# Decode-attention backward: the last quarter of dV of heads 7, 14 and 21 stored as two partition ranges

## The chip, the cores and the metric

The kernel runs on one core of one Trainium2 chip. The metric is the device time of one execution in microseconds (us); lower is better. Times of the kernel before are the median of three runs; the profile is of one further execution, whose own time stands beside its span in the table below.

## The reference

The reference is the forward and backward pass of softmax attention with a single query row per head: 32 heads, 8192 keys, head width 128, everything in bf16.

```python
def _fwd_reference(q, k, v):
    scale = q.shape[-1] ** -0.5
    scores = jnp.einsum('bhqd,bhkd->bhqk', q, k) * scale
    attn = _softmax(scores, axis=-1)
    return jnp.einsum('bhqk,bhkd->bhqd', attn, v)
...
    _out, _vjp = jax.vjp(_f, q, k, v)
    _grads = _vjp(grad_out)
    return (_out0, *[jnp.asarray(_g) for _g in _grads])
```

The shapes are q and grad_out (1, 32, 1, 128), k and v (1, 32, 8192, 128). The outputs are the attention output, dq, dk and dv. Because there is one query row, dv of a head is an outer product, the 8192 softmax weights times the 128 values of grad_out, and dk is the outer product of the 8192 score gradients and q. Each of K, V, dK and dV is 2 MB for a head and 67 MB for all 32 heads, so the kernel must read 134 MB and write 134 MB.

## The kernel before, in words

A head's 8192 rows lie on the 128 partitions, 64 consecutive rows on each, so that one partition holds 64 x 128 bf16, which is 16 KB, contiguous in the chip's main memory too. K, V, dK and dV tiles all have the shape 128 x 64 x 128 and are moved whole: one transfer of 128 rows of 16 KB each. A "quarter" is 16 of the 64 rows of every partition, 128 pieces of 4 KB.

The loop at L307 runs over 33 rounds. Round h computes the forward part of head h (scores from K, softmax, dP from V) and the outer product dv of head h; it also finishes the backward part of head h-1 and the outer product dk of head h-1. `outer` (L250) makes one quarter of such an outer product with one VectorE instruction (L257) into the tile `G`; the tiles G_dv and G_dk have two buffers each, so the VectorE instruction for head h writes a buffer that the store of head h-2 must have left. After the fourth quarter the whole tile is stored with one transfer (L267). Only heads 0 and 31 are stored in two halves.

The order on each engine is the order in which the program is written (a manual schedule). All bulk transfers are issued by SyncE (SP), one after the other; each issue waits for its own condition and holds back those behind it. In a middle round SP issues: `load_k(h + 2)` (L81), the store of dk of head h-1 (L267), `load_v(h + 2)` (L85, written at L387 ahead of the fourth `outer(h, "dv", 3)` at L388), and the store of dv of head h (L267). SP's transfers take eight completion semaphores in turn, so that a transfer also waits until the eighth transfer before it has landed.

Every transfer is spread over the core's 16 DMA engines; each engine works through its own queue of packets in the order of issue, and puts a completion mark of its own on the transfer's semaphore. A transfer has landed when all sixteen marks are there. K tiles have three buffers, V tiles two.

Of the kernel before, what the change touches and what calls it, by code (L numbers as in the profile page):

```python
# [19 lines left out]
K_BUFS = 3  # L20
V_BUFS = 2
QD = 32


@with_exitstack
def kernel(
# [11 lines left out]
    nc = tc.nc  # L38
    P = 128
# [3 lines left out]
    NCH = NT // CH  # L43
    NQ = P // QD
    assert NCH == 4 and NQ == 4
    W = D // 2
    NB = W // QD
    scale = float(D) ** -0.5
# [20 lines left out]
    def rows_of(x, h, c, parts):  # L69
        L = NT // parts  # L70
        return x[0, h].rearrange("(p n) d -> p n d", p=P)[:, c * L:(c + 1) * L, :]

    def slots(X, c, parts):
        L = NT // parts
        return X[:, c * L:(c + 1) * L, :]
# [26 lines left out]
    nc.vector.memset(ones_f[:], 1.0)  # L102
    do_win = consts.tile([P, H, 2, QD + 2], BF16)
    nc.gpsimd.memset(do_win[:], 0.0)  # L104
    wins = {}
    for which in ("p", "ds"):
        wins[which] = []
        for i in range(2):
            w = consts.tile([P, NG, 2 * QD - 4], BF16, name=f"win_{which}{i}")
            nc.gpsimd.memset(w[:], 0.0)  # L110
# [5 lines left out]
    q_blk = consts.tile([P, H, 2 * NB, NQ], BF16)  # L116
    four = consts.tile([H, 2 * NB, NQ, QD], BF16)
    for w in range(NB):
        for e2 in range(2):
            nc.vector.tensor_copy(  # L120
                four[:, 2 * w + e2], rows[:, 0, :].rearrange("h (w j e) -> h w e j", w=NB, e=2)[:, w, e2:e2 + 1, :]
                .to_broadcast([H, NQ, QD]))
    tp = psT.tile([P, 2 * TB, P], BF16, tag="T", name="tp_q")
# [126 lines left out]
    def outer(h, which, r):  # L250
        x = st[h]
        if r == 0:
            x[which] = gpool.tile([P, NT, D], BF16, tag=which, name="G_" + which)
        G, dst = x[which], out_2 if which == "dk" else out_3
        rep, row = x["ds"] if which == "dk" else x["p"], x["qd"][:, 0 if which == "dk" else 1, :]
        Q = NT // 4
        nc.vector.tensor_tensor(  # L257
            slots(G, r, 4).rearrange("p n (a b) -> p n a b", b=R),
            slots(rep, r, 4).unsqueeze(2).to_broadcast([P, Q, D // R, R]),
            row.rearrange("p (a b) -> p a b", b=R).unsqueeze(1).to_broadcast([P, Q, D // R, R]),  # L260
            op=ALU.mult)
        parts = 1
        if h == 0 or h == H - 1:
            parts = 2
        if r % (4 // parts) == 4 // parts - 1:
            c = r // (4 // parts)
            nc.sync.dma_start(rows_of(dst, h, c, parts), slots(G, c, parts))  # L267
# [39 lines left out]
    for h in range(H + 1):  # L307
# [14 lines left out]
        if h > 0:  # L322
            ds_of(p_)
            outer(p_, "dk", 0)
            dq_of(p_, 0)
# [3 lines left out]
        if h > 0:  # L329
            dq_of(p_, 1)  # L330
            outer(p_, "dk", 1)
            if p_ % ST == ST - 1:
                gather_copy("ds")
                gather(p_, "ds", st[p_]["m"])
# [9 lines left out]
        if h > 0:  # L344
            outer(p_, "dk", 2)
# [80 lines left out]
```

## Time and profile before

| what | value |
|---|---|
| median of three runs | 644.06 us (644.03 to 644.63) |
| the profiled execution, its own time | 644.45 us |
| its span, first to last instruction | 642.7 us |
| moved in the span | 269.24 MB, mean 419 GB/s |
| VectorE busy | 537.9 us (84%) |
| TensorE matmul busy | 404.0 us (63%) |
| ScalarE busy | 194.4 us (30%) |
| stores of dv, issue to landing, median | 34.8 us |

The page of a profile gives busy times by engine, then the span cut into 40 slices, the DMA queues, the chain of work that ended last, the costliest groups of instructions and the DMA issues. A view by stretches gives, for any stretch of the span, the mean busy share of the 16 DMA engines and the rate in GB/s; a share of 1.00 means that all sixteen were busy throughout. The trace also keeps the sixteen completion marks of every transfer with their times, without the number of the engine that made them, and the start, length and size of every packet.

### The profile page before, as it was taken

The numbers are of one execution on the slowest core, as the hardware profiler recorded it, in microseconds if no ns is written. First come the engines' busy times: TensorE is split into PE (matmuls) and PEld (weight loads), VectorE is DVE, ScalarE is ACT, GpSimd is POOL, SyncE is SP. The second block draws the span as 40 slices with busy tenths as digits, with TensorE's granted clock in tenths as the row PEclk, the third lists the DMA queues.
The fourth block names the chain that finished last, engine by engine and source line by source line (L and its number), as shares of the span: only waits on it lengthen the run. The fifth ranks groups of instructions, "written<-read, shape, count | busy, mean of one in ns | idle before, by whom it ended". The sixth has DMA issues, their size and how long they took to land.

```text
span 642.7 us, 12069 instructions
## 1 busy us (share of the span) xinstructions
PE 404.0 (63%) x5128; PEld 289.2 (45%) x5128; DVE 537.9 (84%) x780; ACT 194.4 (30%) x475; POOL 5.9 (1%) x11
## 2 busy tenths in 40 slices
PE   2766667776755865458675577645687555765571
PEld 1544445455443543346553445433465343553350
DVE  6899999987988789788798888898878988789871
ACT  2333333332233331234232333213332133331240
POOL 3000000000000000000000000000000000000000
PEclk9888887775778666877577876668866678765775
DMA  8999999999999999999999999999999999999995
GB/s 346 410 428 430 424 428 429 427 425 430 428 425 420 423 426 428 429 429 428 429 430 426 429 430 423 433 428 429 430 423 433 426 428 430 429 428 427 429 390 209
DMA packets 19686, 269.24 MB, mean 419 GB/s; under 512 B 2353, under 2 KB 2353, under 8 KB 2865
## 3 DMA queue, kind: packets, MB, share of 16 engines
q1 hardware_dynamic: 19584, 268.47, 98.4%
q8 instruction: 40, 0.66, 0.4%
q14 instruction: 14, 0.11, 0.0%
q10 hardware_dynamic: 48, 0.01, 0.0%
HBM read 134.23 MB, written 134.23 MB: 418 GB/s over the span
## 4 chain that ended last, share of the span: by engine, by line
DMA 70%; DVE 24%; ACT 2%; PE 1%; issue 1%; POOL 0%; DVEq 0%; POOLq 0%
DMA out_dram<-G_dv 70%; DVE G_dv L257 14%; DVE XK_sb L157 4%; DVE G_dk L257 3%; ACT XV_sb L189 1%; DVE dpT L215 1%; DVE four L120 1%; ACT p_rep L368 0%; DVE sm L174 0%; PE acc_ds L232 0%; POOL do_win L104 0%; PE m_ps L246 0%; PE s_ps L168 0%; DVE ds L288 0%; PE T_ps L198 0%
## 5 line engine op out<-in xcount | busy, mean ns | idle before, releaser
L257 DVE TENSOR_TENSOR G_dv<-p_rep,qd 128x2048 bf16<-128x2048 bf16 x128 | 148.2, 1220 | 54.7 <-DMA out_dram<-G_dv 45.5
L198 PE MATMUL T_ps<-ident_f,Vt 128*128 128x128 f32 x1024 | 162.4, 318 | 0.5 <-DMA Vt<-in_v_dram 0.5
L257 DVE TENSOR_TENSOR G_dk<-ds_rep,qd 128x2048 bf16<-128x2048 bf16 x128 | 155.7, 1219 | 1.2 <-DVE ds_rep L292 0.2
L157 DVE STREAM_TRANSPOSE XK_sb<-Kt 128x1024 f32<-128x1024 f32 x128 | 151.4, 1221 | 4.3 <-DMA Kt<-in_k_dram 4.0
L198 PEld LDWEIGHTS T_ps<-ident_f,Vt 128*128 128x128 f32 x1024 | 144.7, 171 | 17.8 <-ACT XV_sb L189 13.6
L189 ACT COPY XV_sb<-T_ps 128x512 f32<-128x512 f32 x256 | 137.0, 590 | 24.0 <-PE T_ps L198 22.8
L280 PE MATMUL m_ps<-pd,ones_f 128*128 128x1 f32 x64 | 18.7, 361 | 162.9 <-DVE prod L218 162.9
L280 PEld LDWEIGHTS m_ps<-pd,ones_f 128*128 128x128 f32 x64 | 16.0, 311 | 168.8 <-DVE prod L218 154.0
L168 PE MATMUL s_ps<-q_blk,XK_sb 128*128 128x4 bf16 x2048 | 59.8, 168 | 22.9 <-DVE pdt L286 17.6
L168 PEld LDWEIGHTS <-XK_sb 128*128 128x128 bf16 x2048 | 57.1, 104 | 25.8 <-DVE pdt L286 20.2
L232 PE MATMUL acc_ds<-Kt,win_ds 128*32 128x512 bf16 x512 | 67.3, 627 | 0.9 <-ACT win_ds L293 0.9
L293 ACT COPY win_ds<-ds 128x64 bf16<-128x64 bf16 x32 | 7.8, 244 | 197.5 <-DVE ds L288 197.5
L355 ACT ACTIVATE e<-s_ps,nbias 128x64 f32<-128x64 f32 x32 | 10.0, 313 | 133.4 <-DVE nbias L350 133.4
L208 PE MATMUL dp_ps<-XV_sb,do_win 128*32 128x512 bf16 x512 | 34.3, 383 | 24.9 <-ACT XV_sb L189 24.9
L232 PE MATMUL acc_p<-Vt,win_p 128*32 128x512 bf16 x512 | 33.5, 382 | 0.0
L208 PEld LDWEIGHTS <-do_win 128*32 128x32 bf16 x512 | 14.2, 94 | 36.3 <-issue 29.7
L276 ACT CAST qd<-s_ps 128x256 bf16<-128x256 f32 x32 | 11.9, 372 | 43.4 <-PE s_ps L272 43.2
L215 DVE STREAM_TRANSPOSE dpT<-dp_ps 128x512 f32<-128x512 f32 x32 | 21.6, 675 | 0.0
L184 PEld LDWEIGHTS s_ps<-sm,lane 128*32 128x32 f32 x256 | 10.4, 151 | 17.6 <-DVE sm L174 16.7
L343 PEld LDWEIGHTS m_ps<-ident_f,top 128*128 128x128 f32 x32 | 5.8, 182 | 27.3 <-DVE top L341 26.3
L174 DVE TENSOR_TENSOR sm<-s_ps,in_quad 128x256 f32<-128x256 f32 x32 | 13.6, 425 | 4.5 <-PE s_ps L168 2.0
L232 PEld LDWEIGHTS <-win_p 128*32 128x32 bf16 x512 | 10.7, 96 | 12.7 <-ACT win_p L369 2.9
(55 smaller groups left out, 224.0 us busy)
## 6 DMA issues: line engine op xcount, KB each, us to landing
Vt<-in_v_dram SPq DMA_DIRECT2D x32, 2048.0 KB, 32.7
Kt<-in_k_dram SPq DMA_DIRECT2D x31, 2048.0 KB, 30.0
out_dram<-G_dv SPq DMA_DIRECT2D x30, 2048.0 KB, 34.8
out_dram<-G_dk SPq DMA_DIRECT2D x30, 2048.0 KB, 32.3
out_dram<-G_dv SPq DMA_DIRECT2D x4, 1024.0 KB, 13.6
out_dram<-G_dk SPq DMA_DIRECT2D x4, 1024.0 KB, 13.0
Kt<-in_k_dram SPq DMA_DIRECT2D x4, 512.0 KB, 5.2
out_dram<-fin_sb SPq DMA_DIRECT2D x2, 8.0 KB, 13.5
```

The source lines that it names most:

```text
L157: nc.vector.transpose(XK[h][:, :, :, u, :], slots(Kt[h], u, NCH).rearrange("p g d -> p (g d)").bitcast(F32).rearrange("p (g w j) -> p g w ...
L168: nc.tensor.matmul(out[:, g, :], lhsT=cols[:, g, c // 2, c % 2], rhs=q_blk[:, h, c, :], start=(c == 0), stop=(c == 2 * NB - 1), skip_group ...
L174: nc.vector.tensor_tensor(x["sm"][:], x["s"][:, 0:NT].rearrange("p (a g) -> p a g", a=NQ).unsqueeze(2) .to_broadcast([P, NQ, NCH, CH]), in ...
L184: nc.tensor.matmul(x["s"][a * QD:(a + 1) * QD, 128:128 + NT], lhsT=lane[:], rhs=x["sm"][:, a].rearrange("p u g -> p (u g)"), start=True, s ...
L189: nc.scalar.copy(XV[h][:, c * TB:(c + 1) * TB, :], st[h].pop(("T", c))[:])
L198: nc.tensor.transpose(T_ps[:, i, :], words[:, m * P:(m + 1) * P], ident_f[:])
L208: nc.tensor.matmul(out[b * QD:(b + 1) * QD, :], lhsT=do_win[:, h, e2, 2 - 2 * z:2 - 2 * z + QD], rhs=cols[:, z, e2, :, b * QD:(b + 1) * QD ...
L215: nc.vector.transpose(x["dpT"][:].rearrange("p m r -> p (m r)"), x["dp"][:])
L232: nc.tensor.matmul(acc[which][b * QD:(b + 1) * QD, :], lhsT=window(h, which)[:, g, at:at + QD], rhs=X[:, 4 * g:4 * g + 4, :].rearrange("p ...
L257: nc.vector.tensor_tensor(slots(G, r, 4).rearrange("p n (a b) -> p n a b", b=R), slots(rep, r, 4).unsqueeze(2).to_broadcast([P, Q, D // R, ...
L276: nc.scalar.copy(x["qd"][:].rearrange("p a d -> p (a d)"), x["s"][:, 256:512])
L280: nc.tensor.matmul(x["m"][:, 1:2], lhsT=ones_f[:], rhs=x["pd"][:], start=True, stop=True, skip_group_check=True)
```

## The change

For heads 7, 14 and 21 the store of dv is issued in three pieces where it was one. The first three quarters go as one transfer (128 rows of 12 KB) right after the third `outer`, and so before `load_v(h + 2)` in SP's order; the last quarter goes after the fourth `outer` as two transfers over two ranges of partitions: 0 to 118 and 119 to 127 for head 7, 0 to 123 and 124 to 127 for heads 14 and 21, in rows of 4 KB. All other heads, and dk of every head, are stored as before. No compute instruction is changed, and no byte is added.

```diff
+SPLIT = {7: 119, 14: 124, 21: 124}
...
@@ outer
             op=ALU.mult)
+        if which == "dv" and h in SPLIT and r >= 2:
+            if r == 2:
+                nc.sync.dma_start(dst[0, h].rearrange("(p n) d -> p n d", p=P)[:, 0:3 * Q, :], G[:, 0:3 * Q, :])
+            else:
+                c = SPLIT[h]
+                for a, b in ((0, c), (c, P)):
+                    nc.sync.dma_start(rows_of(dst, h, 3, 4)[a:b], slots(G, 3, 4)[a:b])
+            return
         parts = 1
         if h == 0 or h == H - 1:
             parts = 2
```

In the built program the compute engines run the same instructions in the same order. SP issues six more transfers: for head 14, for instance, 128 x 6144 elements of G_dv, then the V load, then 124 x 2048 and 4 x 2048 of G_dv, then the K load.

## Prediction
> **What bounds the kernel now.** I first read the page's strip of DMA and its queues, then the busy share of the DMA engines by stretches towards the end, then SP's own waits, and last the chain through the final 60 us.
>
> ```profile
> span 642.7 us, 12069 instructions
> ...
> DMA  8999999999999999999999999999999999999995
> ...
> DMA packets 19686, 269.24 MB, mean 419 GB/s; under 512 B 2353, under 2 KB 2353, under 8 KB 2865
> ...
> q1 hardware_dynamic: 19584, 268.47, 98.4%
> q8 instruction: 40, 0.66, 0.4%
> ```
>
> The sixteen DMA engines are busy nearly from end to end: the kernel is bound by bytes, and VectorE at 84% is not.
>
> ```profile
> 580.00:600.00 20.00, 12.34 (x158) 8.94 (x158) 16.91 (x25) 5.76 (x14) 0.00 (x0) 0.66 1.01 428
> 600.00:610.00 10.00, 3.51 (x83) 2.71 (x86) 9.59 (x15) 0.62 (x2) 0.00 (x0) 0.57 1.02 433
> ...
> 620.00:626.00 6.00, 3.74 (x31) 1.99 (x27) 5.11 (x11) 1.29 (x5) 0.00 (x0) 0.65 0.92 388
> 626.00:632.00 6.00, 2.16 (x9) 1.88 (x9) 2.31 (x3) 0.81 (x4) 0.00 (x0) 0.50 0.94 393
> 632.00:642.70 10.70, 0.00 (x0) 0.00 (x0) 0.00 (x0) 0.00 (x0) 0.00 (x0) 0.50 0.26 108
> ```
>
> The last two columns are the DMA share and GB/s. To 610 us all engines work; in the last 10.7 us no compute is left and the share is 0.26: some DMA engines are still at it while the others have run out of work. The completion marks say which way. Of dv of head 7 they come from 175.0 to 179.8 us, head 14 from 311.5 to 318.8, head 21 from 447.9 to 457.5, head 30 from 613.3 to 626.7. Always five marks stand together at the front and follow each other every 4.87 us from transfer to transfer; eleven fall behind in jumps of some 1.1 us. One engine is 13.4 us late at head 30 (the next 10). At the end the five put their last mark at 632.5, one at 632.6, nine between 635.7 and 638.2, and the latest at 641.6, 1.1 us before the span ends. The 40 instruction packets took 0.93 to 1.09 us each, about one jump; whether they are the whole cause is not needed here.
>
> ```profile
> SPq L267 <- DVE G_dv L257: 104.8, 33, 16.3
> ...
> SPq L421 <- DMA out_dram<-fin_sb: 12.1, 1, 12.1
> ```
>
> ```profile
> 581.71 34.76 DMA out_dram<-G_dv
> ...
> 616.56 4.63 DVE G_dv L257 x4
> ```
>
> The first fence is from SP's waits (who waited for what: us in total, times, longest), the second from the chain (start, length). SP waits for compute (104.8 us for G_dv alone); no transfer's landing holds it up until the end. The chain's last long pieces: dv of head 29 was issued at 581.71 and landed on its latest engine 34.76 us later, and only then could VectorE write dv of head 31. So the latest engine sets both the last landing and the compute of the tail.
>
> **The change part by part.** *Packet prices.* A 16 KB packet takes 611 ns, an 8 KB one 309, a 4 KB one 159 (medians), and the next starts 4 ns before the last one ends; so 607, 305 and 155 ns apart, and 456 ns for 12 KB by the line between 8 and 16 KB. A mark costs 6 ns. A whole store is 8 rows an engine: 8 x 0.607 + 0.006 = 4.86 us. The three quarters are 8 x 0.456 + 0.006 = 3.65 us. An even quarter would add 8 x 0.155 = 1.24; the cutting alone costs nothing.
>
> *Who gets the last quarter.* No transfer of 119 or 124 rows stands in the trace. In all those that do, the engines get equal parts: 128 rows as 8 on each of 16, 32 rows as 2 each. One bound is therefore an even spread all the same: about 0 us. The other is that an odd number of rows goes to one engine alone: 119 or 124 x 0.155 = 18.4 or 19.2 us on it. Between them lies equal parts over as many engines, up to 16, as divide the number: 119 is 7 x 17, 124 is 4 x 31, 9 is 9 x 1, 4 is 4 x 1. I take that, since it alone keeps what all rows show. The receivers (call them 0 to 3 and 0 to 6) would be the queues that are filled first. Which are those? When the five front engines stand idle at the end, dk of head 31, issued at 626.07, starts on them at 626.91, 626.92, 626.92, 626.95 and 626.97, within 0.06 us. At the start of the kernel, when all sixteen are idle, the first five packets of K come at 2.228, 2.234, 2.237, 2.258 and 2.283, and the sixth only at 2.363. Five queues that start within 0.06 us are there the first five; so I take the front engines as 0 to 4.
>
> The Trainium skill, DMA: Bandwidth & Descriptors, "Why a DMA increments its semaphore by 16 and not by 1", says that a transfer uses the largest count up to 16 that divides the slowest dimension, and, from the SP queue, the lowest-numbered engines; no run here shows it.
>
> *The sum by engine.* Heads 14 and 21: engines 0-3 do 3.65 + 32 x 0.155 + 0.01 = 8.62 us in place of 4.86, +3.76 each time; engines 4-15 do 3.65, -1.21. Head 7: engines 0-6 do 3.65 + 18 x 0.155 + 0.01 = 6.45, +1.59; 7 and 8 do one row, -1.05; 9-15 -1.21. Together: 0-3 +9.1; 4-6 -0.8; 7-8 -3.5; 9-15 -3.6.
>
> *Against the end.* The front engines have put head 30's mark at 613.4; +9.1 is 622.5; then dk 30 (4.87), two halves of dv 31 (4.90) and two of dk 31 (4.90) back to back: 637.2. Before, they lay idle between these. The latest engine: 641.6 - 3.6 = 638.0. So the last landing is 638.0, 3.6 us earlier, if the latest is one of 7-15: nine of the eleven engines that lag. The next, at 638.2, goes to 637.4 at worst. On the way, after head 21, the front engines are 9.1 us later against a gap of 9.6, so no transfer lands later than before.
>
> *SP's order.* The V load of head h+2 now stands behind the three-quarter store, which needs the third outer. For head 14 it goes out near 283.6 in place of 280.96 and lands 3.65 - 1.2 later on the latest engine, at 316.3 in place of 313.8; its first reader, the V transposes, starts at 316.72. Two more transfers use semaphores up, so each waits for one that is two nearer: the 4-row store waits for dk 12 (289.4), and behind it on SP queue the K load (294.05, now 294.2), dk 14 (296.44, now 299.1), the next V load (300.93, now 304.1) and dv 15 (303.88, now 308.9). Up to 5 us late, and all hidden: dv 15's first packet comes at 326.1 on the front engines, 22 us after its issue, because older transfers fill the queues. Without that backlog each such delay would cost up to 5 us. Six more issues at 0.33 us lie in SP's idle time. A late V load would next hold up VectorE, which needs 17.2 us of a round's 19.8 and catches up. I take 0 for all this; bounds 0 and +1 (the V margin of 0.4 gone at three heads).
>
> **Sum.** -3.6 us on a span of 642.7: 639.1, and 640.85 for the profiled execution's 644.45; from the median, 0.4 lower, 640.5. Allowing a tenth for the near tie of 638.0 and 637.2, I say 640.6 us.
>
> **The rivals.**
> *Dearer rows (slower).* Only 512 packets of 4 KB stand in the trace. In the very first K quarter, 8 rows an engine took from 2.23 to 5.2 us in the worst case, 0.37 us a row; when the queues ran, 155 ns. The front engines get 82 such rows. Place: engines 0-3 after head 14, and so dv's landing there, then VectorE. It decides from 0.155 + 4.4/82 = 0.21 us a row on (4.4 is 641.6 - 637.2); at 0.31, 12.7 - 4.4 = 8.3 us slower, 652; at 0.37, 17.6 - 4.4 = 13.2, 657. For it: four engines would walk through 31 rows each out of a tile that otherwise is read by all sixteen evenly. Against: 156 to 159 ns covers half or more of the 4 KB packets.
>
> The Trainium skill, SBUF — State Buffer, "Door 1: The DMA port swizzle", speaks against the change: the port belongs to the partition, not to the engine, so moved rows still pass their own partitions' ports, and ranges 31 apart mostly share one. By it two engines on one port would pay double, 652 as above; by the row it is 640.6, and nothing here shows two engines on one port.
>
> *Wrong receivers (slower).* If the engines that get the quarter are among the eleven that lag, one that ended at 636 goes to 636 + 9.1 = 645.1, 3.5 late: 647.6; were it the latest, 650.7 and 653. For it: engine numbers are not in the trace. Against: the start order above.
>
> *No effect.* Spread evenly all the same, or the latest engine is 5 or 6 (two of eleven, -0.8): 643.3 to 644.2.
>
> **How the numbers follow.** 0.2% is 1.3 us, about what a measurement can tell from no change. Forecast 0.66 (639.8 to 642.5; its own range reaches up, because rows at 0.18 us would bring the front engines to 639.3); no effect 0.11; dearer rows 0.13; wrong receivers 0.10. A little of the no-effect case falls on each side: faster 0.68, same 0.10, slower 0.22. The range runs from 639.6, below which only 3.6 us plus a lucky run would go, to 646.0: it leaves out most of the two slow rivals, about 0.17, and 0.03 below.
>
> **What would show it.** In the changed profile: 124-row and 4-row stores; 384 more packets of 4 KB, still near 159 ns; the share after 632 us near 0.5 in a shorter stretch; the first and last mark of dv 30 within some 4 us of each other (13.4 before); dv 29's landing near 613. It is wrong if the first marks at the end come later than 641, if the 4 KB packets take over 0.21 us, or if marks of dv 14 spread by more than before.

## The result, and the profile after

The changed kernel is slower: 647.27 us against 644.12, a ratio of 1.0047 with the 95% interval 1.0035 to 1.0059. The forecast was 640.6. The profiled execution took 647.49 us, its span is 645.7.

These are lines of the changed kernel's page:

```profile
span 645.7 us, 12081 instructions
...
DMA  8999999999999999999999999999999999999984
...
DMA packets 20101, 269.24 MB, mean 417 GB/s; under 512 B 2384, under 2 KB 2384, under 8 KB 3280
...
q1 hardware_dynamic: 20000, 268.47, 98.1%
q8 instruction: 40, 0.66, 0.4%
```

The bytes are the same and the DMA engines are still busy to the end. Then the stretches at the end (the last two columns are the mean busy share of the sixteen DMA engines and GB/s):

```profile
580.00:600.00 20.00, 11.49 (x155) 8.34 (x158) 16.65 (x24) 5.37 (x14) 0.00 (x0) 0.74 1.01 430
600.00:610.00 10.00, 3.11 (x37) 1.82 (x29) 8.90 (x11) 2.63 (x6) 0.00 (x0) 0.90 0.97 413
610.00:620.00 10.00, 9.31 (x129) 7.06 (x129) 7.80 (x16) 3.58 (x10) 0.00 (x0) 0.59 0.86 367
...
636.00:645.70 9.70, 0.00 (x0) 0.00 (x0) 0.00 (x0) 0.00 (x0) 0.00 (x0) 0.50 0.16 66
```

Before, the share was 1.02 from 600 to 610 us; now it is 0.97 there, 0.86 in the next ten (0.94 before), and 0.16 at the end. The engines run out of work earlier and at more different times: they are less even than before, not more. The completion marks of dv of head 30 say the same: 611.7 to 630.0, a spread of 18.2 us in place of 13.3. The first mark came 1.6 us earlier, the last 3.3 later, and that is about the 3.1 us of the result. At the end eleven engines put their last mark within 0.1 us, at 636.3 to 636.4, and five come later, at 638.0, 639.2, 642.3, 643.6 and 644.8.

The last long pieces of the chain of waits (start, length, what):

```profile
586.11 34.17 DMA out_dram<-G_dv
...
620.37 4.63 DVE G_dv L258 x4
```

It is the chain of before, 3.8 us later: dv of head 29 lands on its latest engine at 620.3 (616.5 before), and only then does VectorE write dv of head 31. SP's own waits (who waited for what: us in total, times, longest) show the eight semaphores at work:

```profile
SPq L269 <- DMA out_dram<-G_dk: 13.1, 3, 4.6
SPq L276 <- DMA out_dram<-G_dk: 11.3, 3, 4.5
SPq L86 <- DMA Kt<-in_k_dram: 11.2, 3, 4.5
```

These are the waits of up to 5 us that were foreseen, three times each; none of them was there before. Of the V transposes' waits the view of the tile Vt has:

```profile
  DMA Vt<-in_v_dram: 7.8, 3
```

That was 0.5 before. So the V load came late to its reader three times, 2.6 us each on average. Whether the time came from there, from the order, from the cut, or from who got the rows, only experiments can say.

### The profile page after: what moved, and what is told of

Its sections match the earlier page's. It is cut to its first block, busy times and chain, and to the rows that moved or that the text cites. A ratio compares the mean times of both kernels' runs of the same rounds, so it can differ in the third digit from the quotient of the medians.

```text
span 645.7 us, 12081 instructions
## 1 busy us (share of the span) xinstructions
PE 403.2 (62%) x5128; PEld 287.2 (44%) x5128; DVE 537.7 (83%) x780; ACT 194.6 (30%) x475; POOL 5.9 (1%) x11
## 2 busy tenths in 40 slices
DMA packets 20101, 269.24 MB, mean 417 GB/s; under 512 B 2384, under 2 KB 2384, under 8 KB 3280
## 4 chain that ended last, share of the span: by engine, by line
DMA 60%; DVE 27%; PE 7%; ACT 2%; issue 1%; POOL 0%; DVEq 0%; POOLq 0%
DMA out_dram<-G_dv 27%; DMA Kt<-in_k_dram 23%; DVE XK_sb L158 10%; DVE G_dv L258 9%; DMA Vt<-in_v_dram 5%; DMA out_dram<-G_dk 5%; DVE G_dk L258 3%; PE s_ps L169 2%; PE acc_ds L233 2%; DVE dpT L216 1%; PE T_ps L199 1%; ACT XV_sb L190 1%; ACT p_rep L377 1%; DVE four L121 1%; DVE prod L219 1%
## 5 line engine op out<-in xcount | busy, mean ns | idle before, releaser
L258 DVE TENSOR_TENSOR G_dk<-ds_rep,qd 128x2048 bf16<-128x2048 bf16 x128 | 155.7, 1218 | 1.1
```

The lines of the kernel that those rows point to most:

```text
L258: nc.vector.tensor_tensor(slots(G, r, 4).rearrange("p n (a b) -> p n a b", b=R), slots(rep, r, 4).unsqueeze(2).to_broadcast([P, Q, D // R, ...
```

## The experiments

Every experiment is a whole kernel. Those with an interval were timed against the kernel before on the same chip; its median was 644.1 to 644.2 throughout.

### Which engines take part: a probe

The kernel before with one tiny load behind the store of dv in rounds 1 to 30:

```diff
+    probe = consts.tile([16, H, 8], BF16)
...
+        if 1 <= h <= 30:
+            n = (h - 1) % 15 + 1
+            nc.sync.dma_start(probe[0:n, h, :], k[0, 0].rearrange("(p n) d -> p n d", p=P)[0:n, 0, 0:8])
```

Expected: 

> The kernel before, plus one tiny load in each of rounds 1 to 30 (n pieces of 16 bytes on n partitions, n = 1 to 15 and again, right behind the store of dv), whose completion marks tell which DMA engines took part. If a transfer of n rows goes to the n lowest-numbered engines and the five engines that never lag are engines 0 to 4 (the prediction's step), the marks of n = 1 to 5 all stand with the front group of the neighbouring store's marks, within 0.3 us of its first, and the marks that lag come in from n = 6 on. If the receivers are engines that lag (the rival), marks several us behind the front appear already at n = 1 to 4, the engine that lags most is among 1 to 7, and the front group fills up only at n of 8 and more. Time within 1 us of the kernel before.

Measured: 644.25 us (one run). A probe of n rows left n marks of engines, besides one that comes at the issue. Its marks lie some 0.2 us (0.17 to 0.24) behind marks of the neighbouring store, so a probe can be laid over the store's sixteen and the engine that n adds to n-1 read off. I number the engines from 0 in the order in which n brings them in. From the second pass, in us behind the store's first mark:

```
 n  head  marks of the probe
 1   16   0.81
 2   17   1.30 2.15
 3   18   0.75 0.89 1.55
 4   19   0.88 0.93 1.54 3.51
 5   20   0.72 0.77 1.16 3.10 6.80
 7   22   0.53 0.60 1.19 3.14 3.59 3.85 7.35
 8   23   0.29 0.56 0.60 1.19 3.60 3.87 3.96 7.85
 9   24   0.31 0.58 0.65 0.74 1.23 3.74 3.89 4.06 8.22
12   27   0.34 0.63 0.67 0.78 1.82 3.66 3.92 3.99 4.03 5.01 7.23 9.17
15   30   0.34 0.65 0.71 0.78 1.85 5.01 5.23 5.32 5.46 5.51 5.55 5.79 6.49 7.20 10.31
```

The sets are nested: n rows go to n engines, and each n keeps those of n-1. Engines 0 and 2 belong to the front; 1 is a microsecond or so behind; 3 is in the middle; n = 5 brings in the engine that is latest of all; 5 and 6 are in the middle; n = 8 and 9 bring in two more of the front; n = 12 the second latest. The store's first mark, at 0.00, has no partner even at n = 15, so it is engine 15. The front is 0, 2, 7, 8 and 15, not 0 to 4; the latest is engine 4, one of head 7's receivers.

### The same cut, spread evenly

The changed kernel with other numbers:

```diff
-SPLIT = {7: 119, 14: 124, 21: 124}
+SPLIT = {7: 64, 14: 64, 21: 64}
```

Expected: 

> The changed kernel with 64 and 64 partitions in place of 119 and 9 or 124 and 4: the same cut into three pieces, the same order and semaphores, the same 4 KB rows, but each half is spread over all sixteen engines. If the loss comes from which engines get the last quarter (theory), it is gone: 644.1 us, within 0.6. If it comes from the cut itself (SP's order, the semaphores used up, the V load behind the store, 4 KB rows), it stays: 646.5 to 647.5.

Measured: 645.21 us, ratio 1.0014 (1.0005 to 1.0022). This lies between the two theories: 2.1 of the 3.1 us go away when nobody gets more than the others, and 1.1 stay.

### One head at a time

Five kernels that differ from the changed one in this line alone:

```diff
-SPLIT = {7: 119, 14: 124, 21: 124}
+SPLIT = {21: 124}
+SPLIT = {7: 119}
+SPLIT = {7: 124}
+SPLIT = {14: 124, 21: 124}
+SPLIT = {7: 125}
```

Head 21 alone. Expected: 

> The changed kernel with head 21 alone cut (124 and 4). Theory: engines 0 to 3 get 3.76 us more and the others 1.21 less. In the changed kernel the last mark of dv of head 30 was at 630.0 on an engine that had received 9.1 us, so without any it would stand at 620.9; with 3.76 it is at 624.7, and the engine that was latest before (626.7) is relieved to 625.5 if it is none of 0 to 3: 642.9 us, 1.2 faster than before. If it is one of 0 to 3, 648 us. If the cut itself costs, a third of 3.1: 645.1.

Measured: 643.58 us, ratio 0.9991 (0.9982 to 1.0000), 0.56 faster, with an interval that just reaches no change. Half of the 1.2 came.

Head 7 alone, as in the change. Expected: 

> The changed kernel with head 7 alone cut (119 and 9). Theory: engines 0 to 6 get 1.59 us more. If the engine that lags most is one of them, the end moves by that: 645.7 us. If it is one of 7 to 15, it is relieved by 1.05 to 1.21 and the time is 643.0. If the cut itself costs, a third of 3.1: 645.1.

Measured: 645.96 us, ratio 1.0025 (1.0016 to 1.0034), 1.8 slower. In its trace the last mark goes from 179.0 at the V load to 186.7 at the next K load, 7.7 us for one transfer that takes 4.87, and the rest is the 17 and 1 rows: 18 x 0.155 + 0.01 = 2.8.

Head 7 with the numbers of the others. Expected: 

> The changed kernel with head 7 alone cut, but at 124 and 4 instead of 119 and 9. Theory: head 7 at 119 lost because engine 4, the latest, was one of its seven receivers; at 124 the receivers are 0 to 3, engine 4 is relieved, and the time is that of head 21 alone: 643.6, within 0.5. Rival: an early cut loses because of its place in the run, whoever receives: 645.5 to 646.2, as at 119.

Measured: 643.48 us, ratio 0.9989 (0.9980 to 0.9998), 0.63 faster: the place is not what matters. The same head loses 1.8 us with 119 rows and gains 0.6 with 124, because 119 has engine 4 among its receivers and 124 has not.

Heads 14 and 21, head 7 whole. Expected: 

> The changed kernel with heads 14 and 21 cut (124 and 4) and head 7 stored whole. The probe puts engines 0 and 2 in the front group, engine 1 about a microsecond behind it, engine 3 among the many in the middle, engine 4 last of all. Theory: what decides is the latest engine. Before, engine 4 put its last mark of dv of head 30 at 626.7 and the middle ones theirs at 620.9 to 622.1; two cuts give engine 3 2 x 3.76 = 7.5, so 628.4 to 629.6, later than engine 4: 1.7 to 2.9 slower than before, 645.8 to 647.0. Rival: each cut at 124 is worth what head 21 alone was worth, 0.56 less: 643.0.

Measured: 645.95 us, ratio 1.0023 (1.0014 to 1.0032), 1.8 slower. The twelve runs lie wide, from 644.11 to 647.12 with four of them below 645, where head 21 alone had 643.39 to 644.43; the profiled one took 646.35. One cut gains and two lose: in the profile the last mark of dv of head 30 stands at 628.8, inside the 628.4 to 629.6 that engine 3 was to reach. Its chain has dv of head 29 landing at 619.2 (584.97 + 34.19), where one cut at head 21 has it at 615.7 (580.80 + 34.89) and the kernel before at 616.5:

```profile
584.97 34.19 DMA out_dram<-G_dv
...
619.25 4.63 DVE G_dv L258 x4
```

And the same line with head 21 alone:

```profile
580.80 34.89 DMA out_dram<-G_dv
...
615.78 4.63 DVE G_dv L258 x4
```

Head 7 with one row more. Expected: 

> The changed kernel with head 7 alone cut, at 125 and 3 (at 124 and 4 it was 643.48). 125 = 5 x 25: if the receivers are engines 0 to 4, the latest engine, number 4, now does 3.65 + 25 x 0.155 + 0.01 = 7.54 in place of 4.86 us, 2.7 more where 124 relieved it by 1.2: 644.1 + 2.7 + 0.35 for the cut, 646.8 to 647.2. If who receives does not matter, or the latest engine is another: 643.5 as with 124, or up to 644.5.

Measured: 646.97 us, ratio 1.0045 (1.0031 to 1.0059), as the theory had it. Going from 124 to 125 rows costs 3.5 us, because 125 = 5 x 25 takes engine 4 in. How many engines take part is to be read in the page's packets, since every engine of a transfer writes one mark of 4 bytes. With 125 and 3:

```profile
DMA packets 19821, 269.24 MB, mean 417 GB/s; under 512 B 2360, under 2 KB 2360, under 8 KB 3000
```

Two heads at 124 and 4:

```profile
DMA packets 19957, 269.24 MB, mean 418 GB/s; under 512 B 2368, under 2 KB 2368, under 8 KB 3136
```

A kernel without any cut (the one with swapped order below) has 2352 packets under 512 B. 125 and 3 add 8 = 5 + 3; two times 124 and 4 add 16 = 4 x 4; the changed kernel's 2384 is 32 more, 7 + 9 + 4 x 4.

The engines can also be followed through a trace. A packet starts 4 ns before the one ahead of it on the same engine ends, and every engine takes the transfers in the order of issue, so the packets of one engine can be strung together, with the times of the marks as a control. In the changed kernel the last mark of dv of head 30, at 630.0, stands on a string that carried 31 rows of 4 KB at heads 14 and 21 and 17 at head 7, so it is one of engines 0 to 3. The mark before it, at 628.6, stands on one that carried 17 rows and none of the 31: by its lag this is engine 4. With heads 14 and 21 cut the latest string carried 31 rows twice, with 125 and 3 it carried the 25 rows, and with head 21 alone it carried none.

### What the even cut still costs

The cut in two instead of three, with the quarter in one piece of 128 rows:

```diff
-SPLIT = {7: 119, 14: 124, 21: 124}
+SPLIT = {7: 0, 14: 0, 21: 0}
...
-                for a, b in ((0, c), (c, P)):
+                for a, b in ((c, P),):
```

Expected: 

> The changed kernel with the last quarter in one piece of 128 rows (three quarters, V load, quarter; heads 7, 14, 21), spread over all sixteen engines. The even cut in three pieces cost 1.07 us for three heads, where the packets explain 0.2. If the third transfer and its semaphore cost, 644.3. If the order (three-quarter store ahead of the V load) or the shorter rows cost, 645.2 as with three pieces.

Measured: 645.11 us, ratio 1.0014 (1.0006 to 1.0023). The third transfer and its semaphore cost nothing that shows (0.1 us); 1.0 us is left for the order or the shorter rows.

The same two pieces, both issued behind the fourth outer, so that the V load stands ahead of them as it did before (an edit of the kernel before):

```diff
+        if which == "dv" and h in (7, 14, 21):
+            if r == 3:
+                nc.sync.dma_start(dst[0, h].rearrange("(p n) d -> p n d", p=P)[:, 0:3 * Q, :], G[:, 0:3 * Q, :])
+                for a, b in ((0, P),):
+                    nc.sync.dma_start(rows_of(dst, h, 3, 4)[a:b], slots(G, 3, 4)[a:b])
+            return
```

Expected: 

> Heads 7, 14 and 21 cut into three quarters and a quarter of 128 rows, both issued behind the fourth outer, so that the V load stands ahead of both as in the kernel before. The same cut with the V load between the pieces cost 1.0 us. If the order cost it: 644.1 to 644.4. If the cut into shorter rows did: 645.1.

Measured: 644.24 us, ratio 0.9998 (0.9989 to 1.0007). The shorter rows cost nothing that shows.

Nothing cut, the order alone changed:

```diff
-        if 0 < h and h + 2 < H:
+        if 0 < h and h + 2 < H and h not in (7, 14, 21):
             load_v(h + 2)
         outer(h, "dv", 3)
-        if h == 0:
-            load_v(2)
+        if h in (0, 7, 14, 21):
+            load_v(h + 2)
```

Expected: 

> The kernel before with nothing cut, but at heads 7, 14 and 21 the V load stands behind the whole store of dv. If the order alone costs: 645.1. If not: 644.1 to 644.4.

Measured: 645.86 us, ratio 1.0027 (1.0018 to 1.0036): 1.7 us for three swaps, more than was expected. Part of it can be seen in the trace. In SP's order before, loads and stores of 2 MB take turns. With the V load behind the store of dv, that store follows the store of dk directly. At head 14 of the swapped kernel the latest engine's marks go from 309.0 (dk) to 314.3 (dv), 5.3 us; in the kernel before, behind the V load, the same store took 5.0 (313.8 to 318.8). The packets that fill this stretch, one after the other on one engine, took 700, 738 and 733 ns where 16 KB otherwise take 611. In the changed kernel's three-quarter stores the same stands: at head 14, from 311.59 on, 12 KB packets of 559, 564 and 559 ns in a row, where the median is 460. With the V load first they took at most 485 to 493.

There is a rival: the V load, now behind the store, also comes late to its reader. In the swapped kernel's page the V transposes wait 12.6 us for it (the last figures of the line), where it was 0.5 before:

```profile
L198 PE MATMUL T_ps<-ident_f,Vt 128*128 128x128 f32 x1024 | 169.1, 327 | 12.6 <-DMA Vt<-in_v_dram 12.6
```

This is not what costs. Strung together, the packets of the latest engine follow each other without a gap from 60 to 613 us, before as in the swapped kernel, so that engine never waited for work. What grew is its packets of 16 KB: beyond 611 ns each, they took 11.6 us in sum before and 13.2 in the swapped kernel, and the last mark of dv of head 30 moved from 626.7 to 628.1. The three stores that follow a store have 0.8 us of this, the rest is spread over other transfers. Why a store behind a store runs slow on the engine that comes last stays open.

### Can it be had faster?

Two cuts at 123 and 5, of the last 13 rows of each partition, with the V load first:

```diff
+        if which == "dv" and h in (14, 21):
+            if r == 3:
+                rows = dst[0, h].rearrange("(p n) d -> p n d", p=P)
+                nc.sync.dma_start(rows[:, 0:51, :], G[:, 0:51, :])
+                for a, b in ((0, 123), (123, P)):
+                    nc.sync.dma_start(rows[a:b, 51:NT, :], G[a:b, 51:NT, :])
+            return
```

Expected: 

> The kernel before with dv of heads 14 and 21 stored, behind the fourth outer and the V load as ever, as 51 of the 64 rows of every partition and then the other 13 rows as 123 and 5 partitions. If a transfer of 123 = 3 x 41 rows goes to engines 0, 1 and 2, these (the front two and the one close behind them) get 8 x 0.494 x 51/52 + 42 x 0.127 + 0.02 - 4.86 = 4.3 us more at each head and the others, engine 3 too, 0.85 to 1.0 less: engine 4 ends dv of head 30 at 626.7 - 1.7 = 625.0, engine 1 at 616.3 + 8.6 = 624.9. So 1.7 faster, 642.4; 643.1 if the cut costs as much a head as the even cut did (0.36). If it is not those three, 644.1 or more.

Measured: 643.43 us with runs from 642.37 to 645.8, ratio 0.9991 (0.9981 to 1.0000). The 1.7 us did not come. At head 14 the packets of 3.25 KB took up to 918 ns (median 131) and some 13 KB ones beside them 650 to 1218 (median 488); at head 21 there is next to nothing of this. That the pieces hold each other up when nothing stands between them is not shown: with three quarters and a quarter behind the V load nothing stands between them either, and there no 12 KB packet took over 493 ns. The long packets stay unexplained.

Head 21 alone at 124 and 4, with the V load first; against the edit with two pieces and the V load first:

```diff
-        if which == "dv" and h in (7, 14, 21):
+        if which == "dv" and h in (21,):
...
-                for a, b in ((0, P),):
+                for a, b in ((0, 124), (124, P)):
```

Expected: 

> Head 21 alone, 124 and 4, but with the V load ahead of all pieces as in the kernel before (with the V load between them it was 643.58). If the order costs 0.35 a head: 643.0 to 643.3. If the pieces get in each other's way when nothing stands between them, as the longer packets in the 123 and 5 run suggest: 643.6 to 644.3.

Measured: 643.22 us, ratio 0.9985 (0.9976 to 0.9994). This is 0.97 us faster than the kernel before and 4 faster than the changed one: a single cut with the V load first beats both. Against the same cut with the V load between the pieces it is 0.36 faster, which the two intervals do not tell apart. The runs lie from 642.78 to 644.31; the profiled one took 644.0, and its span of 642.2 us is 0.5 less than before.

## Why the prediction was wrong

**The latest engine sets the end: right.** In the profiles the time follows the last mark of dv of head 30: 626.7 before, 630.0 changed, 628.8 with two cuts, 625.8 with head 21 alone.

**Packet prices and equal parts: right.** 4 KB packets kept their median of 159 ns (mean 174 to 176 at heads 7 and 14, 159 at head 21), so "dearer rows" is out: it needed 0.21 us a row on all 82. The marks of 4 bytes show 7, 9, 4 and 4 engines, as equal parts would have it. The prediction's estimate from the SBUF ports, double the price for ranges 31 apart, is not borne out by these packets. What the Trainium skill's page DMA: Bandwidth & Descriptors says under "Why a DMA increments its semaphore by 16 and not by 1", that a transfer from the SP queue goes to the lowest-numbered engines, fits the probe: its sets are nested from n = 1 to 15, though the marks carry no numbers of their own.

**The step that failed: "so I take the front engines as 0 to 4".** It rested on start times: five idle engines that begin within 0.06 us at the end, and five first packets within 0.06 us at the kernel's start. The changed kernel shows that this tells nothing: there eleven engines have no older work left at the end, and all eleven begin dk of head 31 within 0.13 us (630.73 to 630.86). Engines that are idle start together, whichever they are. The probe has the front as 0, 2, 7, 8 and 15. With that map the prediction's own sums give the end of engine 3: in the middle, it ended dv of head 30 at 620.9 to 622.1 before; +9.1 is 630.0 to 631.2, and the last mark stands at 630.0. The rival "wrong receivers" had this, with 647.6 for an engine of the middle, and was given 0.10. The string of packets shows that the latest engine is one of 0 to 3, by its 31, 31 and 17 rows; that it is number 3 follows, since 0 and 2 were in the front and 1 close behind them.

That this rival comes so near the 647.3 is partly luck, because the sums do not give engine 4. It was to be relieved of 3.6 in the prediction, by the right map of 0.8, to 625.9; it ended at 628.6, 1.9 later than before. So by this profile the change would have lost time even if engine 3 had been in the front. The order accounts for 1.0 of the 2.7 us between 625.9 and 628.6 (next paragraph), and 0.6 stood in this one profile ahead of head 7 already; the rest is open.

**The second term that was off: SP's order, taken as 0 with bounds 0 and +1.** It is worth 1.0 to 1.1 of the 3.1 us, at the upper bound, and by another way than was thought. The V load did come late to its reader (7.8 us of wait in three places, 0.5 before), and the semaphores did hold SP up by as much as 4.6, but the third transfer, which is what uses the semaphores up, can go without changing the time, and the queues of the two latest engines never ran dry (0.01 us of gaps in sum from 60 to 613 us). What costs is the order: with it restored the same cut is free (0.9998), and the order without a cut costs 1.7. Slower packets in a store that directly follows a store are 0.8 us of that in the trace; the rest of the way is not shown.

**The sum.** Order 1.0; the rest, 2.1, is the rows given to engines 0 to 6 and 0 to 3. The parting is not exact, since the order without a cut cost 1.7. For head 7 alone: +1.6 on engine 4, and a third of 1.0 for the order, is 1.9; 1.8 was measured. For one cut at 124: -1.2 + 0.35 is -0.85; -0.56 and -0.63 were measured. With the order restored it is -1.2; -0.97 was measured.

## What to carry to other kernels

Where transfers are the bound, look at the sixteen completion marks of a transfer and not only at its landing: the latest engine is what the kernel waits for. Before work is shifted between DMA engines, find out by a probe which engine is which; a count that divides the number of rows decides who takes part, and one row more or less (124 or 125) changed the time by 3.5 us. An uneven spread pays while the receivers stay ahead of the latest engine, and turned into a loss here where one of them passed it, so the slowest receiver sets the dose. When a store is split, keep loads and stores in turn.

## What the runs showed of the hardware

The sixteen DMA engines of the core did not end together though every transfer was spread evenly: in 613 us engine 4 fell 13.3 us behind engines 0, 2, 7, 8 and 15, engine 11 some 10, engine 1 some 3, the other eight 7.5 to 9.

The strings of packets of the kernel before show two causes. The 40 instruction packets of 16 KB took 0.88 to 1.09 us each. From 60 us on they stand in the strings of eight engines, four or five in each, in the place of a data packet: each starts 4 ns before a data packet ends, and the next data packet of that engine starts about when it is done. That is some 5 us of the lag of these eight, and it is where the prediction's jumps of some 1.1 us come from. The latest engine, number 4, has none of them: its data packets themselves are slower, 624 ns on average for 16 KB over 889 packets where a front engine has 612, which makes 11 us. Why they are slower stays open.

Two 2 MB stores issued one behind the other ran slower on that engine: the second took 5.3 us where it took 5.0 to 5.1 behind a V load (at head 14 packets of 700 to 738 ns for 611). Three such places make 0.8 us of the 1.7 by which that kernel was slower.
